# Loads, transform order and weight products at the head of a Fourier-mixing and leaky-ReLU kernel

## The chip, the cores and the metric

The kernel runs on one core of one Trainium2 chip. The metric is the time on the device in microseconds (us) for one launch. Times with L and a number refer to lines of the kernel before; TensorE is PE in the profile (its weight loads are PEld), VectorE is DVE, ScalarE is ACT, GpSimd is POOL and SyncE, which issues the DMAs, is SP.

## What is computed

The reference takes x of 8 batches of 3008 x 256 in fp32, forms the real part of its two-dimensional Fourier transform in each batch, and sends the 24064 rows of 256 through two weight matrices with a leaky ReLU between:

```python
X = np.fft.fft(x, axis=1)                 # x: (8, 3008, 256)
X = np.fft.fft(X, axis=2).real.astype(np.float32)
h = X.reshape(24064, 256) @ w_in          # (256, 2048)
g = np.maximum(0.01 * h, h)
out = g @ w_out                           # (2048, 256)
```

Both weight matrices come as 64-bit floats, and the kernel turns them into 32-bit floats itself.

## The kernel before, in words

**Stages.** The transform along the 256 features is never done on x. It is multiplied into the weights: a "weight product" (`fold_w_in`, L388) multiplies the table of feature cosines and sines (`feat_sb`) with w_in and leaves `wf`, whose two planes belong to the cosine and the sine part. The sequence transform remains. It uses mirror symmetries: `add_mirrors` (L241) adds a row block and its mirror image, `fold_columns` (L247 for the cosine part, L249 and a small memset at L250 for the sine part) folds the feature halves onto each other, and `fold_halves` (L257) adds or subtracts the halves of the sequence, for the even or odd output parity. What is left are small matmuls against tables: `sequence` (L416) does four with even rows (L431, 95 of the 128 partitions carry rows) and three with odd rows (L441). `butterfly` (L446) then combines the even and odd sums into the mixed rows: one copy on ScalarE (L452) and four operations on VectorE (L453 to L457). Feature column 128 has no partner; its transform (`nyquist`, from `nyx`, which holds all eight batches) goes the same way for 8 rows at once and is then spread over all partitions: for the first block by a matmul with a row of ones (`spread_first`, L516, and copies at L517), later through DRAM. For output parity 0 the rows are folded once more into quarters (`fold_quarters`, L274 to L280, six operations on VectorE and two copies on ScalarE).

**Blocks.** A batch and a parity make a unit; its 753 or 752 mixed columns are cut into three blocks of 251 or 250. For each block `up` (L532) multiplies by `wf` into two PSUM tiles, cos_ps and sin_ps (L538), VectorE adds the column-128 part and forms sums and differences (L543, L547, L548), and ScalarE applies the leaky ReLU (L549). `down` multiplies by w_out: `down_plain` (L581) for the first two blocks, a form with seven products in place of eight (L601), with sums made by GpSimd (L556 to L559), for all others. There are 48 blocks of 8 steps.

**The head.** Weights and the first batch arrive while the kernel already runs. Up to step 15 the order on VectorE, TensorE and SyncE is written out by hand (`manual_schedule`, L652), in an inner region on GpSimd too; ScalarE's order and everything after step 15 is placed by the framework's scheduler, which may also put later operations into earlier gaps. SyncE issues the DMAs of the head in one queue, at most eight in flight. `keep_warm` (L646) issues matmuls on zeros. A block of weights is converted in several VectorE operations, interleaved with the steps: `begin` (L343, L344, then L345 and L346 on ScalarE), `mantissa` (L351), `end` (L361, L362). w_in comes as 256, 256 and three times 512 columns, so there are five weight products; each writes its planes in PSUM tiles of the tag "up", of which there are four shared with cos_ps, sin_ps and the transforms, and ScalarE copies them to `wf` (L394). After the copy of the plane w=1, SyncE spreads one row of it to `wn` (L401), which L543 needs.

**The places that the steps touch.** In the inner region (L663 to L704): loads of x split into `evens` (four of seven row groups) and `odds`; fillers, Nyquist additions on GpSimd (L482 to L484), conversion and first weight product, fillers, column-128 transform, then row folds on VectorE, transforms of the first unit, spreading, and the first butterfly. Behind it the hand-written steps: `up(*steps[n])`, `down(*steps[n-2])`, conversions, and the weight products 2 to 5. [...]

Of the kernel before, what the change touches and what calls it, by code (L numbers as in the profile page):

```python
# [55 lines left out]
P = 128  # L56
# [3 lines left out]
NT = 7  # L60
# [144 lines left out]
def tile_fnet_leaky_relu(  # L205
# [99 lines left out]
    def load_tab(q, n, c):  # L305
        t = const.tile([P, TW[c][n % 2]], F32, name=f"tab_{n}_{c}")
        q.dma_start(t, seq_tab[n, c, :, 0 : TW[c][n % 2]])
        tabs[n, c] = t
# [79 lines left out]
    def fold_w_in(f0, n, made):  # L388

        for w in (1, 0):  # L390
            pt = up_ps()[:, 0:n]
            for a in range(2):
                nc.tensor.matmul(pt, lhsT=feat_sb[:, a, w * P : (w + 1) * P], rhs=made[a].dst, start=(a == 0), stop=(a == 1))  # L393
            nc.scalar.copy(wf[:, w, f0 : f0 + n], pt)  # L394
            if w == 1:
                spread_wn(f0, n)
# [19 lines left out]
    def sequence(rows, m, part, c):  # L416
# [3 lines left out]
        pe, po = dft_ps(), dft_ps()  # L420
        kf, kw = KF[c], KW[c]
        tab, n = tabs[2 * part, c], NI[0]
        for i in range(n):
            if c == 1:
                still, to = rows[0:PE_ROWS, i], pe[0:m, i % 2 * kf : (i % 2 + 1) * kf]
            else:
# [5 lines left out]
                             start=(i == 0), stop=(i == n - 1), skip_group_check=True)  # L432
        tab, n, at = tabs[2 * part + 1, c], NI[1], 0
# [10 lines left out]
        return pe, po  # L444
# [14 lines left out]
    def dft(u, blk):  # L459


        b, c = u
        if u in folded:
            rows = folded[u][blk]
        elif c == 1:
            rows = zs[b][:, 1 - blk, 0, :, blk * P : (blk + 1) * P]
        else:
            rows = quarters.pop((b, blk))
        sums = sequence(rows, P, blk, c)

        def rest():
            t = work.tile([P, UW[0]], F32, tag=f"mix{blk}", bufs=2, name=f"mix{blk}")
            butterfly(t, sums, P, blk, c)
            mixed.setdefault(u, {})[blk] = t
        return rest
# [10 lines left out]
    def nyquist(c):  # L486
        if c == 1:
            rows = nya[:, 1]
        else:
            halves = [nyb[:, 0], nyb[:, 1]]  # L490
            fold_quarters(nya[:, 0], halves, halves[0][:, 5], [h[:, 6] for h in halves])
            rows = halves, halves[0][:, 5]
        sums = sequence(rows, B, 0, c)

        def rest():
            t = work.tile([P, UW[0]], F32, tag="mix0", bufs=2, name="nyq")
            butterfly(t, sums, B, 0, c)
            nc.sync.dma_start(nyq_dram[:, c, 0 : UW[c]], t[0:B, 0 : UW[c]])
            return t
        return rest  # L500
# [116 lines left out]
    def step(at):  # L617
        if at < len(steps):
# [6 lines left out]
            if n == 0 and f in (2, 5):  # L625
                dft(units[1], f // 5)()
            if 0 < n < len(units) - 1 and f == 4:
# [4 lines left out]
                else:  # L632
                    dft(units[n + 1], part - 1)()
# [7 lines left out]

    def convert_w_in(f0, n, made):
        convert(made)
        fold_w_in(f0, n, made)
# [7 lines left out]
    with tc.manual_schedule(engines={mybir.EngineType.DVE, mybir.EngineType.PE, mybir.EngineType.SP}):  # L652
        with tc.manual_schedule(engines={mybir.EngineType.Pool}):
# [10 lines left out]

            def load_rows(h, rows):
                nc.sync.dma_start(t[:, h, :, rows], x[0, :, h, :, rows])
# [3 lines left out]
            load_rows(0, evens)  # L670
            nc.sync.dma_start(feat_sb, feat_tab.rearrange("(a p) n -> p a n", p=P))
            load_rows(1, evens)
            nc.sync.dma_start(nyx, x_nyq)
            for n in range(2):
                load_tab(nc.sync, n, 1)
            for h in range(2):
                load_rows(h, odds)
            for n in range(2, 4):
                load_tab(nc.sync, n, 1)
            o = load_w_out(0)  # L680
            keep_warm(10)
            fold_nyquist()
            convert_w_in(0, half, w)
            w, w1 = load_w_in(half, half), load_w_in(WN, WN)
            keep_warm(7)
            differences = work.tile([P, 4 * CW], F32, tag="s", bufs=4, name="differences")[:, 0 : NT * P].rearrange("p (c d) -> p c d", c=NT)
            nyq = nyquist(1)
            for rows in (evens, odds):
                for h in range(2):
                    add_mirrors(t, h, rows)  # L690
                    fold_columns(t, h, 0, rows)
                    if rows == odds and h == 0:
                        fold_columns(t, h, 1, slice(0, NT))
                fold_halves(t, 0, 1, rows, differences)
            fold_columns(t, 1, 1, slice(0, NT))
            fold_halves(t, 1, 1, slice(0, NT))
            zs[0] = t
            folded[units[0]] = differences, t[:, 0, 0, :, P:D]
# [96 lines left out]
```

## Time and profile before

The three timed runs have a median of 1932.13 us (1931.54 to 1933.2). The profiled execution has a span of 1930.8 us (1932.87 as timed). Its start, read from the timeline of the trace:

| what | start, us | length, us |
|---|---|---|
| fillers (L650), first piece | 1.09 | 6.08 |
| first weight product (L393) | 8.92 | 1.97 |
| fillers, second piece | 10.72 | 3.19 |
| column-128 transform (L431, then L441) | 13.84 | 1.44, then 2.06 from 15.12 |
| cosine rows, even (L431) | 17.11 | 1.54 |
| cosine rows, odd (L441) | 20.59 | 3.48 |
| sine rows, even (L431) | 23.86 | 1.82 |
| sine rows, odd (L441) | 25.52 | 2.06 |
| spreading (L516) | 27.51 | 1.52 |
| first product of the first block (L538) | 28.96 | 1.11 |

The weight products start at 8.92, 39.07, 51.88, 71.54 and 96.30 us. The transform of column 128 for parity 0 stands at 121.15 us on TensorE.

How to read it: lengths overlap, since matmuls are pipelined and their modelled ends lie after the start of the next. An fp32 matmul is two passes in the profile, so 8 passes are 4 matmuls. A time in square brackets behind a line is how long the engine had stood idle before it, and what ended that. "PEclk" is the clock granted to TensorE as a share of the full one. In the view by stretches the columns are busy time and number of instructions of each engine, then PEclk, the busy share of the DMA engines and the GB/s.

### The profile page before, as it was taken

Reading aid. Unit: us, or ns where it says so; the run is one execution under the profiler, and the core shown is the slowest. Engines: PE = TensorE matmul, PEld = TensorE weight load, DVE = VectorE, ACT = ScalarE, POOL = GpSimd, SP = SyncE. Lnnn points to the kernel's source line nnn. Section 1 sums busy time; section 2 is a strip of 40 time slices with the busy share of each in tenths; the row PEclk is TensorE's granted clock in tenths of the full one; section 3 lists DMA queues with packets and bytes.
Section 4 is the critical chain, followed back from the end, with each engine's and each line's share of the span. In section 5 each row is a group of like instructions: output and inputs, shape, how many; then the busy total and the mean of one; then the engine's idle time right before and its main releaser. Section 6 shows DMA issues by size and latency. Waiting matters only on the chain.

```text
span 1930.8 us, 24800 instructions
## 1 busy us (share of the span) xinstructions
PE 1918.1 (99%) x9040; PEld 1692.8 (88%) x9040; DVE 1157.2 (60%) x2273; ACT 468.7 (24%) x552; POOL 1061.4 (55%) x1513
## 2 busy tenths in 40 slices
PE   8999999999999999999999999999999999999999
PEld 6788888888888888888888888888888888888888
DVE  7868555584555755567555775558655585555554
ACT  3522222222222222222222222222222222222221
POOL 0136555575555755557555665556655575555554
PEclk9999999999999999999999999999999999999999
DMA  6202000110002000020000200002000020000000
GB/s 247 77 31 96 11 20 22 36 71 11 20 22 88 19 12 30 12 95 12 22 19 11 95 23 11 19 12 95 22 11 19 12 106 11 19 11 22 11 12 22
DMA packets 26728, 73.29 MB, mean 38 GB/s; under 512 B 4832, under 2 KB 17760, under 8 KB 24816
## 3 DMA queue, kind: packets, MB, share of 16 engines
q1 hardware_dynamic: 26608, 71.72, 10.0%
q8 instruction: 72, 1.18, 0.3%
q14 instruction: 48, 0.39, 0.1%
HBM read 46.99 MB, written 24.71 MB: 37 GB/s over the span
## 4 chain that ended last, share of the span: by engine, by line
PE 95%; DVE 3%; DMA 1%; issue 1%; ACT 0%; SPq 0%; DVEq 0%; ACTq 0%
PE sum_ps L601 55%; PE cos_ps L538 16%; PE sin_ps L538 16%; PE dft_ps L441 3%; PE sum_ps L581 3%; PE dft_ps L431 2%; DMA xt<-in_x_dram 1%; PE up_ps L393 1%; DVE cos L543 0%; DVE g L547 0%; DVE xt L241 0%; DVE g L548 0%; DVE xt L257 0%; DVE xt L247 0%; DVE xt L249 0%
## 5 line engine op out<-in xcount | busy, mean ns | idle before, releaser
L543 DVE SCALAR_TENSOR_TENSOR cos<-nb,wn,cos_ps 128x251 f32<-128x251 f32 (+1 forms) x768 | 330.6, 472 | 676.6 <-PE cos_ps L538 675.5
L549 ACT ACTIVATE g<-g 128x1004 f32<-128x1004 f32 (+1 forms) x384 | 399.2, 1040 | 1196.4 <-DVE g L548 1099.2
L556 POOL TENSOR_TENSOR s<-g 128x251 f32<-128x251 f32 (+1 forms) x368 | 268.1, 729 | 736.0 <-ACT g L549 736.0
L601 PE MATMUL sum_ps<-s,wt 128*128 128x251 f32 (+1 forms) x2208 | 528.0, 374 | 0.0
L601 PEld LDWEIGHTS sum_ps<-s,wt 128*128 128x128 f32 x2208 | 415.5, 188 | 53.2 <-issue 0.7
L538 PE MATMUL cos_ps<-mix,wf 128*128 128x251 f32 (+1 forms) x1536 | 388.4, 375 | 2.6 <-ACT wf L394 2.6
L538 PE MATMUL sin_ps<-mix,wf 128*128 128x251 f32 (+1 forms) x1536 | 387.8, 374 | 0.0
L601 PE MATMUL sum_ps<-g,wo 128*128 128x251 f32 (+1 forms) x1472 | 372.0, 374 | 0.8 <-DVE o L612 0.8
L538 PEld LDWEIGHTS cos_ps<-mix,wf 128*128 128x128 f32 x1536 | 290.8, 190 | 40.2 <-ACT wf L394 5.5
L538 PEld LDWEIGHTS sin_ps<-mix,wf 128*128 128x128 f32 x1536 | 290.4, 189 | 34.7
L601 PEld LDWEIGHTS sum_ps<-g,wo 128*128 128x128 f32 x1472 | 279.2, 190 | 40.6 <-DVE o L612 1.6
L559 POOL TENSOR_TENSOR s<-g,s 128x251 f32<-128x251 f32 (+1 forms) x368 | 273.2, 742 | 28.9
L547 DVE TENSOR_TENSOR g<-cos,sin_ps 128x502 f32<-128x502 f32 (+1 forms) x384 | 259.7, 676 | 47.0 <-DVE cos L543 10.3
L557 POOL TENSOR_TENSOR s<-s,g 128x251 f32<-128x251 f32 (+1 forms) x368 | 275.1, 748 | 0.0
L558 POOL TENSOR_TENSOR s<-g 128x251 f32<-128x251 f32 (+1 forms) x368 | 261.8, 712 | 0.0
L548 DVE TENSOR_TENSOR g<-cos,sin_ps 128x502 f32<-128x502 f32 (+1 forms) x384 | 257.2, 670 | 0.0
L601 PE MATMUL sum_ps<-s,wo 128*128 128x251 f32 (+1 forms) x736 | 215.8, 375 | 0.0
L601 PE MATMUL sum_ps<-g,wt 128*128 128x251 f32 (+1 forms) x736 | 215.8, 375 | 0.0
L601 PEld LDWEIGHTS sum_ps<-s,wo 128*128 128x128 f32 x736 | 139.5, 189 | 16.3
L601 PEld LDWEIGHTS sum_ps<-g,wt 128*128 128x128 f32 x736 | 139.8, 190 | 15.8
L612 DVE TENSOR_TENSOR o<-e,sum_ps 128x251 f32<-128x251 f32 (+1 forms) x184 | 67.5, 408 | 8.7 <-ACT e L610 8.7
L581 PE MATMUL sum_ps<-g,wo 128*128 128x251 f32 x256 | 57.1, 374 | 0.0
(75 smaller groups left out, 677.6 us busy)
## 6 DMA issues: line engine op xcount, KB each, us to landing
xt<-in_x_dram SPq DMA_DIRECT2D x14, 1792.0 KB, 9.3
out_dram<-o SPq DMA_DIRECT2D x80, 251.0 KB, 2.3
raw<-in_w_out_dram SPq DMA_DIRECT2D x8, 512.0 KB, 4.4
out_dram<-o SPq DMA_DIRECT2D x16, 250.0 KB, 2.1
raw<-in_w_in_dram SPq DMA_DIRECT2D x6, 512.0 KB, 4.4
nb<-nyq_dram SPq DMA_DIRECT2D x8, 376.5 KB, 3.4
nb<-nyq_dram SPq DMA_DIRECT2D x7, 376.0 KB
xt<-in_x_dram SPq DMA_DIRECT2D x2, 1024.0 KB, 7.6
```

Source lines behind the costliest of these rows:

```text
L538: nc.tensor.matmul(pt[blk][:, h * n : (h + 1) * n], lhsT=wf[:, blk, fs[h] * P : (fs[h] + 1) * P], rhs=mixed[b, c][blk][:, at : at + n], st ...
L543: nc.vector.scalar_tensor_tensor(cos[:, hs], in0=spreads[b, c][:, at : at + n], scalar=wn[:, fs[h] : fs[h] + 1], in1=pt[0][:, hs], op0=ALU ...
L547: nc.vector.tensor_tensor(g[:, 0], cos[:, 0 : 2 * n], pt[1][:, 0 : 2 * n], op=ALU.add)
L548: nc.vector.tensor_tensor(g[:, 1], cos[:, 0 : 2 * n], pt[1][:, 0 : 2 * n], op=ALU.subtract)
L549: nc.scalar.activation(g, g, ACT.Lrelu)
L556: nc.gpsimd.tensor_tensor(s1, a[1][0], a[1][1], op=ALU.add)
L557: nc.gpsimd.tensor_tensor(s2, s1, a[0][0], op=ALU.subtract)
L558: nc.gpsimd.tensor_tensor(s3, a[0][0], a[1][0], op=ALU.subtract)
L559: nc.gpsimd.tensor_tensor(s4, a[0][1], s2, op=ALU.subtract)
L581: nc.tensor.matmul(sums[j][d][:, r * n : (r + 1) * n], lhsT=wo[:, fs[h] // NH, fs[h] % NH, d * P : (d + 1) * P], rhs=a[r][h], start=(f == ...
L601: nc.tensor.matmul(sums[j][p], lhsT=still[p], rhs=moving[p], start=(f == 0 and i % 2 == 0), stop=(f == NH - 1), skip_group_check=True)
L612: nc.vector.tensor_tensor(to, x, y, op=ALU.add)
```

## The change

1. **Fewer bytes.** Of the even rows of the first batch and of the even tables only 96 of 128 partitions are loaded; GpSimd sets the other 32 partitions of the even rows to zero.
2. **Load order.** w_in, both even halves, the first even table, the feature table, column 128, both odd halves, the other three tables, w_out.
3. **Order in the head.** The Nyquist additions and the conversion come first, then all row folds on VectorE, with the sine folds of the even rows moved ahead of the odd rows. On TensorE the fillers are one piece of 20, before 10 and 7. Then even rows of column 128, even rows of the cosines, the first weight product, and after it the odd rows of both, then the sines. The weight product thus stands in the middle of the column-128 (d=128) transform; its PSUM tiles are now of the tag "sum". The loads of the next w_in blocks stay behind the weight product in SyncE's queue.
4. **Pieces.** Each weight product's plane w=0 is computed and copied in two pieces of half the columns, in one PSUM tile; the plane w=1 stays whole.
5. **Places of the weight products.** The fourth (from column 1024) moves from behind down(5) to before it, right behind up(7); the fifth moves from the start of step 12 to step 11, between up(11) and down(9).
6. **Tail.** Both `fold_halves` for parity 0 stand at step 14, before one each at 14 and 15. The quarter folds of the first batch and of column 128 for parity 0 are now the last things in the hand-written order.

The functions `sequence`, `dft` and `nyquist` are split so that the even and the odd rows can be called apart; the operations stay the same.

```diff
+    def load_tab(n, c):
+        rows = slice(0, (PE_ROWS + 1) if n % 2 == 0 else P)
         t = const.tile([P, TW[c][n % 2]], F32, name=f"tab_{n}_{c}")
-        q.dma_start(t, seq_tab[n, c, :, 0 : TW[c][n % 2]])
+        nc.sync.dma_start(t[rows], seq_tab[n, c, rows, 0 : TW[c][n % 2]])
...
-    def fold_w_in(f0, n, made):
-        for w in (1, 0):
-            pt = up_ps()[:, 0:n]
-            for a in range(2):
-                nc.tensor.matmul(pt, lhsT=feat_sb[:, a, w * P : (w + 1) * P], rhs=made[a].dst, start=(a == 0), stop=(a == 1))
-            nc.scalar.copy(wf[:, w, f0 : f0 + n], pt)
+    def fold_w_in(f0, n, made, tag="up"):
+        for w, pieces in ((1, 1), (0, 2)):
+            pt = ps.tile([P, 512], F32, tag=tag, bufs=4, name="wf_ps")
+            for piece in range(pieces):
+                cols = slice(piece * n // pieces, (piece + 1) * n // pieces)
+                for a in range(2):
+                    nc.tensor.matmul(pt[:, cols], lhsT=feat_sb[:, a, w * P : (w + 1) * P], rhs=made[a].dst[:, cols],
+                                     start=(a == 0 and piece == 0), stop=(a == 1), skip_group_check=True)
+                nc.scalar.copy(wf[:, w, f0 + cols.start : f0 + cols.stop], pt[:, cols])
...
+            nc.gpsimd.memset(t[PE_ROWS + 1 : P, :, :, evens], 0.0)
             def load_rows(h, rows):
-                nc.sync.dma_start(t[:, h, :, rows], x[0, :, h, :, rows])
+                used = slice(0, PE_ROWS + 1 if rows == evens else P)
+                nc.sync.dma_start(t[used, h, :, rows], x[0, used, h, :, rows])
...
             w = load_w_in(0, half)
-            load_rows(0, evens)
+            for h in range(2):
+                load_rows(h, evens)
+            load_tab(0, 1)
             nc.sync.dma_start(feat_sb, feat_tab.rearrange("(a p) n -> p a n", p=P))
-            load_rows(1, evens)
             nc.sync.dma_start(nyx, x_nyq)
-            for n in range(2):
-                load_tab(nc.sync, n, 1)
             for h in range(2):
                 load_rows(h, odds)
-            for n in range(2, 4):
-                load_tab(nc.sync, n, 1)
+            for n in range(1, 4):
+                load_tab(n, 1)
             o = load_w_out(0)
-            keep_warm(10)
             fold_nyquist()
-            convert_w_in(0, half, w)
-            w, w1 = load_w_in(half, half), load_w_in(WN, WN)
-            keep_warm(7)
+            convert(w)
...
-            nyq = nyquist(1)
             for rows in (evens, odds):
                 for h in range(2):
                     add_mirrors(t, h, rows)
                     fold_columns(t, h, 0, rows)
                     if rows == odds and h == 0:
-                        fold_columns(t, h, 1, slice(0, NT))
+                        fold_columns(t, h, 1, rows)
                 fold_halves(t, 0, 1, rows, differences)
-            fold_columns(t, 1, 1, slice(0, NT))
+                for h in range(2):
+                    if rows == evens or h == 1:
+                        fold_columns(t, h, 1, rows)
             fold_halves(t, 1, 1, slice(0, NT))
...
-            ready = [nyq, dft(units[0], 0), dft(units[0], 1)]
-            spread_first(ready[0]())
-            ready[1]()
+            keep_warm(20)
+            cosine, sine = ((rows_of(units[0], blk), P, blk, 1) for blk in range(2))
+            nyq = nyquist_rows(1), B, 0, 1
+            evens = [even_rows(*nyq), even_rows(*cosine)]
+            fold_w_in(0, half, w, "sum")
+            w, w1 = load_w_in(half, half), load_w_in(WN, WN)
+            sums_of_d128 = evens[0], odd_rows(*nyq)
+            sums_of_cosines = evens[1], odd_rows(*cosine)
+            sums_of_sines = even_rows(*sine), odd_rows(*sine)
+            spread_first(mix_nyquist(1, sums_of_d128))
+            mix(units[0], 0, sums_of_cosines)
             o.begin()
             o.mantissa()
-            ready[2]()
+            mix(units[0], 1, sums_of_sines)
...
         up(*steps[7])
+        fold_w_in(2 * WN, WN, w2)
         down(*steps[5])
-        fold_w_in(2 * WN, WN, w2)
...
-            if at == 12:
-                fold_w_in(3 * WN, WN, w3)
             if old is not None:
                 convert_on(old, new)
             up(*steps[at])
+            if at == 11:
+                fold_w_in(3 * WN, WN, w3)
             down(*steps[at - 2])
-            if at > 13:
-                fold_halves(t, at - 14, 0, slice(0, NT))
+            if at == 14:
+                for part in range(2):
+                    fold_halves(t, part, 0, slice(0, NT))
         done = 14
-    for part in range(2):
-        fold_x_quarters(0, part)
-    nyquist(0)()
+        for part in range(2):
+            fold_x_quarters(0, part)
+        nyq = nyquist_rows(0), B, 0, 0
+    mix_nyquist(0, (even_rows(*nyq), odd_rows(*nyq)))
```

## The prediction

> **What bounds the kernel now.** First the page, for the share of each engine; then the chain of waits over the first 160 us, for what sets the time where TensorE isn't full; then the timeline for each step of the change; then the stretch table for clock and bandwidth.
>
> ```profile
> PE 1918.1 (99%) x9040; PEld 1692.8 (88%) x9040; DVE 1157.2 (60%) x2273; ACT 468.7 (24%) x552; POOL 1061.4 (55%) x1513
> ```
>
> TensorE is busy all the time, and the change removes no useful matmul: it touches only the first 125 us. What it can win there is TensorE's idle and half-speed time, plus its filler matmuls; beyond, the chain is matmuls back to back, and any shift of the head reaches the end one to one. The chain shows where the head isn't matmul-bound:
>
> ```profile
> 15.84 0.97 DVE xt L241
> ...
> 20.59 3.48 PE dft_ps L441 x6
> 24.07 1.61 PE dft_ps L431 x8
> 25.68 1.90 PE dft_ps L441 x6
> 27.58 1.47 PE dft_ps L516 x4
> ...
> 71.70 3.45 PE up_ps L393 x8
> 75.17 0.59 ACT wf L394
> 75.81 1.11 PE cos_ps L538 x4
> ```
>
> Up to 20.6 us the last rows of x set the pace (the DMA before the first line ends at 15.8); then the transforms; and after each weight product (L393) TensorE waits for ScalarE's copy (L394). In the first L441 line six passes of 376 columns take 3.48 us; the third line shows 1.90 for the same six. The reason is in the stretch table (PEclk is the column after the busy times):
>
> ```profile
> 20.00:21.00 1.00, 0.41 (x2) 0.32 (x3) 1.00 (x2) 0.00 (x0) 0.00 (x0) 1.00 1.11 398
> 21.00:22.00 1.00, 1.00 (x4) 0.52 (x3) 0.90 (x2) 0.00 (x0) 0.00 (x0) 0.61 1.06 424
> 22.00:23.00 1.00, 1.00 (x3) 0.66 (x2) 1.00 (x3) 0.00 (x0) 0.00 (x0) 0.50 1.03 420
> ```
>
> After 1.94 us of idling the clock falls to half for about 3.4 us. The timeline gives the rest:
>
> ```profile
> 11.38 1.23 DVE L241 TENSOR_TENSOR xt<-xt 128x1024 f32<-128x1024 f32 x1 [1.28 <-DMA xt<-in_x_dram]
> 11.72 1.16 POOL L482 TENSOR_TENSOR nyx<-nyx 128x112 f32<-128x112 f32 x1 [10.54 <-DMA nyx<-in_x_nyq_dram]
> ...
> 20.59 3.48 PE L441 MATMUL dft_ps<-tab,differences 128*128 128x376 f32 x6 [1.94 <-DVE differences L257]
> ...
> 28.96 1.11 PE L538 MATMUL cos_ps<-mix,wf 128*128 128x251 f32 x4
> ...
> 68.14 3.56 PE L581 MATMUL sum_ps<-g,wo 128*128 128x251 f32 x16
> ...
> 70.97 0.69 DVE L362 SCALAR_TENSOR_TENSOR win<-win,power 128x512 f32<-128x512 f32 x1
> ...
> 71.54 3.59 PE L393 MATMUL up_ps<-win,feat_sb 128*128 128x512 f32 x8
> ```
>
> The fourth line is the first block's first product: its start, 28.96 us, measures the head. The last three matter most below: the third weight product starts right as its weights are finished on VectorE.
>
> **What the Trainium skill says.** (1) "TensorE: Matmul & The Clock Gate", Part 1, "What's actually happening": half rate after an idle window of about 3.4 us, full rate after a busy one, windows running freely. The trace agrees on the length (0.5 from 21.4 to 24.6), but idling 1.94 us was enough; 1.75 us before 8.92 was not. (2) "PSUM — Partial Sum Buffer", "PSUM bank collisions raise a hardware error": two engines must be kept apart by bank, not by address. The trace agrees as far as it goes: at 101.72 L543 begins on the first half of cos_ps only when both halves, in one bank, are done (100.57 + 1.11 = 101.68). (3) "DMA: Bandwidth & Descriptors", "Why a DMA increments its semaphore by 16 and not by 1": a 96-partition tile still goes to 16 engines. No run here shows such a load. (4) "SBUF — State Buffer", "Who interferes with whom": GpSimd and VectorE can lock each other out. L482 agrees: 1.16 us for 112 elements, ending 0.27 after L241, where its neighbours of 56 take 0.30.
>
> **The change part by part.** All from the profiled execution, whose span is 1930.8 us; the timed runs lie at 1932.13 (1931.54 to 1933.2). I add the difference to 1932.13.
>
> *Loads.* Each evens load falls from 1024 to 768 KB (96 of 128 rows), each even table from 376 to 282. Behind one another up to: evens 1280 and 2048 KB, first table 2330, nyx 2698, odds 3466 and 4234, second table 4798 (before: nyx 2928, odds 4636 and 5404). The stretch table has some 410 GB/s, 400 KB a us, from 8 us on. From the old ends (evens 1536 KB at 8.14, nyx 2928 at 11.72, odds 4636 at 15.84): evens 7.5 and 9.4, nyx 11.15, odds 13.1 and 14.8, second table 16.2. GpSimd's new memset writes 4096 elements on 32 partitions; `blank` took 0.31 for 256 and `one` 0.20 for 128, so about 3.5 us, over by 4.8, before anyone needs it; it only sits ahead of the Nyquist additions, which wait for 11.15. Bounds: 0, or 1.7 us later if rows rather than bytes set the load time (rival 3).
>
> *VectorE.* Conversion unchanged, ended 7.2. Then with the durations of the timeline (1024: 1.25, 768: 1.0, 512: 0.62, 384: 0.5): evens end 11.3, cosine difference 11.9, sine columns 13.1; odds 0 to 15.1; odds 1 and difference 17.1; sine halves 18.6. Before, the difference ended at 20.4 and sine at 22.5. Splitting two sine folds (2 x 1.0 into 2 x 0.62 + 2 x 0.48) adds 0.2, hidden in the wait for odds.
>
> *TensorE.* The 27 fillers become 20 in one piece, to 1.09 + 6.0 + 20 passes x 0.213 = 11.3. Nyquist additions end near 12.3 (three of 0.3 from 11.15, and turns with VectorE). From 12.4 all is there in time, so the chain is a sum: three even transforms at 1.28, three odd at 1.99, weight product 1.80, spreading 1.45 = 13.06, plus 0.62 for the cut product: its two pieces lie in one PSUM tile, so by (2) the second waits for the copy of the first (end of matmul 0.18, copy of 128 columns 0.26 by 0.37 for 256 and 0.59 for 512, signals 0.09, restart 0.09). The first block begins at 26.1 instead of 28.96: **-2.85**. No 1.9 us gap is left. The first L543 follows by 1.2, as before. Bounds -1 and -3.3. SP's weight loads, now behind the later wn copies, land before 24; w[0].begin wants them near 25.7. Hidden.
>
> *Second and third product (L393 at 39.07 and 51.88).* Before, the copy costs 0.80 and 0.95 (51.88 + 3.42 = 55.30 without it; 56.16, and 0.09 for the restart). Now a wait of 0.62 or 0.73 lies between the pieces, and ScalarE has its 0.72 us conversions (L345, L346) in the way. I take 0 for both; bounds -0.9 and +0.6 each.
>
> *Fourth product (w2), moved ahead of down(5).* VectorE's work isn't moved: w2[1] ends at 71.66, and VectorE has no idle from 57.31 to there. TensorE's up(7) ends at 68.14, where down(5) now hides the wait. After the change the product starts at 68.14, does the half with w2[0] to 69.0, and waits for w2[1] to 71.7: **2.7 us idle**, with down(5) queued behind. Counted from up(4) at 56.16: 15.55 to the weights, then 0.85 + 0.85, 0.73 between pieces, 0.85, down(5) 3.40: up(8) after 22.2 instead of 19.65 + 0.09: **+2.5** (+1.8 if pieces overlap). By (1) a gap longer than 1.94 should also halve the clock for 3.4 us; with 0.6 of that waiting, **+1.4** (0 to 1.7).
>
> *Fifth product (w3), moved to up(11).* Its weights end at 92.0, up(11) at 92.9: no wait. 0.95 becomes 0.73: -0.2 (bound -0.95).
>
> *Tail of the head.* Both sine and cosine halves at step 14 fall into VectorE's idle (2.87 and 1.00 us before 111.91 and 117.01). The Nyquist quarter folds, six of 0.16 at 13.6 to 15.4 now, come last in VectorE's written order. I take 0, if TensorE's order puts the block's next product first; bound below. Even tables of the second parity: fewer bytes, no waiter, 0.
>
> Sum: -2.85 + 0 + 2.5 + 1.4 - 0.2 = **+0.85**: 1933.0.
>
> **Rivals.** *1, faster: pieces overlap, clock stays.* For it: the columns are disjoint, and the gap may straddle two windows. Against: shared tile, and the 20.6 us gap. Head -3.45, second -0.8, third -0.95, fourth +1.85, fifth -0.95: -4.3, so 1927.8. *2, slower: the Nyquist transform of the even parity starves.* TensorE does it at 121.15, between steps 15 and 16. VectorE is full from 117.0; its last quarter fold ends at 122.87 and six Nyquist folds now follow, to about 123.3. If the order on TensorE stays, it idles 2.15 and the clock falls, 1.4: 1936.6. It decides when the folds end over 2 us after step 15. For it: the order in this trace. Against: code after the written-out region is placed by readiness, and up(16) could go first. *3: the change doesn't do what it says.* 96 rows take as long as 128, the head gains nothing, and the fourth product still costs: 1935.9. For it: six rows an engine is an untried shape; against: (3).
>
> **How the numbers follow.** Forecast 0.5 (own range 1930.5 to 1935.0); rival 1 0.17, rival 2 0.18, rival 3 0.15. About 0.2%, 3.9 us, is what a measurement can tell from no change. Below 1928.3 lies most of rival 1, with partly hidden copies: 0.14. Above 1936.0: most of rival 2, half of 3: 0.18. The rest, 0.68. The range 1928.0 to 1936.8 takes in the rivals but their outer halves.
>
> **What would show it.** Head: L538 first at 26.1, L441 on the differences near 1.9 us, and PEclk 1.0 there. Product: a PE wait on ScalarE inside L393. Fourth product: 2.7 us of TensorE waiting for L362, then clock 0.5. Nyquist: a wait for L280 near 118. I am wrong if that 2.7 us wait isn't there, or if the head gains under 1 us.

## The result, and the profile after

The changed kernel takes **1941.64 us** (median of four runs, 1940.83 to 1942.47) against 1932.66 (1931.54 to 1933.63) before: a ratio of 1.0047, 95% interval 1.0029 to 1.0064. It is some 9 us **slower**, and outside the range of the prediction (1933.0; 1928.0 to 1936.8). The profiled execution has a span of 1940.1 us, 9.3 over the one before.

From here on L numbers are those of the changed kernel: products L397 and their copies L399 (were L393, L394), even rows L435 (L431), odd rows L450 (L441), column-128 additions L491 to L493 (L482 to L484), the block's products L544 (L538), end of a weight conversion L363 (L362). Runs built on the kernel before have its numbers, shifted by what they add.

The page's first section shows a busy TensorE as before; 6.4 us more of it, and 26 more instructions:

```profile
PE 1924.5 (99%) x9066; PEld 1699.3 (88%) x9066; DVE 1158.1 (60%) x2275; ACT 468.8 (24%) x557; POOL 1064.3 (55%) x1516
```

A matmul counts as longer when the clock is low, so this row doesn't say what was lost. The chain of waits does (start, length, what):

```profile
3.76 10.09 DMA nyx<-in_x_nyq_dram
...
13.99 0.73 POOL nyx L491
...
14.79 0.64 POOL nyx L492
15.43 0.04 issue
15.47 5.48 PE dft_ps L435 x16
20.96 2.57 PE wf_ps L397 x8
...
25.01 4.08 PE dft_ps L450 x12
29.09 1.28 PE dft_ps L435 x8
```

Before, rows of x set the pace. Now one transfer of 112 KB, column 128, is under way for 10.09 us, and TensorE's first transform waits for it and for the two additions. The prediction had that transfer landing at 11.15 and the transform starting at 12.4; it started at 15.47. Then sixteen passes of L435 take 5.48 us, where eight take 1.28 further down: half speed again. The stretch table (columns as before) has both causes:

```profile
9.00:10.00 1.00, 1.00 (x6) 0.87 (x6) 0.96 (x2) 0.00 (x0) 0.00 (x0) 1.00 1.02 244
10.00:11.00 1.00, 1.00 (x7) 0.87 (x6) 0.58 (x1) 0.00 (x0) 0.00 (x0) 1.00 1.03 210
...
14.00:15.00 1.00, 0.00 (x0) 0.00 (x0) 1.00 (x2) 0.00 (x0) 0.92 (x2) 0.77 1.04 421
15.00:16.00 1.00, 0.53 (x2) 0.24 (x3) 1.00 (x3) 0.00 (x0) 1.00 (x2) 0.50 1.02 415
...
24.00:25.00 1.00, 1.00 (x5) 0.87 (x6) 0.00 (x0) 0.00 (x0) 0.00 (x0) 0.61 0.07 1
```

From 5 to 12 us, while the 96-row loads run, the DMA engines are as busy as ever (1.02) and move only 184 to 250 GB/s; from 13 to 18 us, with the odd rows on all partitions, they move 396 to 432. And from about 14.5 (0.77 over its slice) to 24.8 (0.61) the clock is at half: ten microseconds, where before it was 3.4. The timeline shows where the first block and the fourth weight product now stand:

```profile
15.47 2.68 PE L435 MATMUL dft_ps<-tab,nyx 95*8 95x188 f32 x8 [3.91 <-POOL nyx L492]
...
33.65 1.11 PE L544 MATMUL cos_ps<-mix,wf 128*128 128x251 f32 x4
...
74.01 1.12 PE L397 MATMUL wf_ps<-win,feat_sb 128*128 128x512 f32 x2
77.98 2.42 PE L397 MATMUL wf_ps<-win,feat_sb 128*128 128x512 f32 x6 [2.85 <-DVE win L363]
80.86 2.07 PE L397 MATMUL wf_ps<-win,feat_sb 128*128 128x256 f32 x4 [0.46 <-ACT wf L399]
```

Each row below takes the starts of two products of a block (the step's number in brackets) in both traces:

| stretch on TensorE | before | after | difference | predicted |
|---|---|---|---|---|
| start to up(0) | 28.96 | 33.65 | +4.69 | -2.85 |
| up(0) to up(2), second product | 12.62 | 12.79 | +0.17 | 0 |
| up(2) to up(4), third product | 14.58 | 15.21 | +0.63 | 0 |
| up(4) to up(7) | 10.28 | 10.51 | +0.23 | 0 |
| up(7) to up(8), fourth product | 9.37 | 14.02 | +4.65 | +3.9 |
| up(8) to up(11) | 15.39 | 15.28 | -0.11 | 0 |
| up(11) to up(12), fifth product | 9.37 | 9.58 | +0.21 | -0.2 |
| up(12) to the end | 1830.2 | 1829.1 | -1.1 | 0 |

The last row holds +0.3 around the column-128 transform, and the absence of two delays that the trace of before has, 0.8 us near 179 us and 0.6 us near 1118 us. Most other traces, those of x7, x11 and y1 among them, lack both delays too. So some 1.4 us by which such a run is shorter than before says nothing of its edit.

### The profile page after: what moved, and what is told of

The parts are those of the page before. It is cut to its first block, busy times and chain, and to the rows that moved or that the text cites. A ratio compares the mean times of both kernels' runs of the same rounds, so it can differ in the third digit from the quotient of the medians.

```text
span 1940.1 us, 24859 instructions
## 1 busy us (share of the span) xinstructions
PE 1924.5 (99%) x9066; PEld 1699.3 (88%) x9066; DVE 1158.1 (60%) x2275; ACT 468.8 (24%) x557; POOL 1064.3 (55%) x1516
## 3 DMA queue, kind: packets, MB, share of 16 engines
q1 hardware_dynamic: 26352, 70.90, 10.2%
## 4 chain that ended last, share of the span: by engine, by line
PE 97%; DVE 1%; DMA 1%; ACT 0%; SPq 0%; issue 0%; POOL 0%; DVEq 0%; POOLq 0%; ACTq 0%
PE sum_ps L607 56%; PE cos_ps L544 17%; PE sin_ps L544 17%; PE dft_ps L450 3%; PE sum_ps L587 2%; PE dft_ps L435 2%; PE wf_ps L397 1%; DMA nyx<-in_x_nyq_dram 1%; DMA wn<-wf 0%; DVE g L553 0%; DVE cos L549 0%; DVE g L554 0%; ACT wf L399 0%; ACT g L555 0%; DVE win L363 0%; DVE power L362 0%
## 5 line engine op out<-in xcount | busy, mean ns | idle before, releaser
L544 PE MATMUL cos_ps<-mix,wf 128*128 128x251 f32 (+1 forms) x1536 | 388.2, 375 | 0.0
L544 PE MATMUL sin_ps<-mix,wf 128*128 128x251 f32 (+1 forms) x1536 | 387.8, 374 | 0.0
L544 PEld LDWEIGHTS cos_ps<-mix,wf 128*128 128x128 f32 x1536 | 291.0, 190 | 35.0 <-issue 0.6
L544 PEld LDWEIGHTS sin_ps<-mix,wf 128*128 128x128 f32 x1536 | 290.4, 189 | 34.7
L563 POOL TENSOR_TENSOR s<-s,g 128x251 f32<-128x251 f32 (+1 forms) x368 | 279.5, 759 | 0.0
L554 DVE TENSOR_TENSOR g<-cos,sin_ps 128x502 f32<-128x502 f32 (+1 forms) x384 | 257.2, 670 | 0.0
```

The costliest lines, as they stand in the source:

```text
L544: nc.tensor.matmul(pt[blk][:, h * n : (h + 1) * n], lhsT=wf[:, blk, fs[h] * P : (fs[h] + 1) * P], rhs=mixed[b, c][blk][:, at : at + n], st ...
L554: nc.vector.tensor_tensor(g[:, 1], cos[:, 0 : 2 * n], pt[1][:, 0 : 2 * n], op=ALU.subtract)
L563: nc.gpsimd.tensor_tensor(s2, s1, a[0][0], op=ALU.subtract)
```

## The experiments

Most variants were run once, and the time stands beside that of the kernel before on the same chip, in brackets. Twenty runs of the kernel before spread over 3 us (1931.33 to 1934.54) and sixteen of y1 over 5, so a difference of 1 or 2 us between single totals says little. The argument rests on the starts in the traces.

**The load rate alone (x4_rates).** Kernel before, with the later batches' loads each cut in two by partitions:

```diff
-            nc.sync.dma_start(t[:, h], x[b, :, h])
+            if b == 1:
+                nc.sync.dma_start(t[0:96, h], x[b, 0:96, h])
+                nc.sync.dma_start(t[96:P, h], x[b, 96:P, h])
...
+            elif b == 3:
+                nc.sync.dma_start(t[0:112, h], x[b, 0:112, h])
+                nc.sync.dma_start(t[112:P, h], x[b, 112:P, h])
...
+            else:
+                nc.sync.dma_start(t[:, h], x[b, :, h])
```

> The kernel before, with the loads of the later batches of x, which are off the path, cut by partitions: batch 1 in 96 and 32 rows, batch 2 in 64 and 64, batch 3 in 112 and 16, batch 4 in 80 and 48, batch 5 in 32 and 96 (from partition 32), batches 6 and 7 whole. Each has the same bytes. Theory A (which partitions a transfer reaches sets its rate, not its bytes): whole batches land at 400 GB/s in 8.5 to 9 us for 3.6 MB, batch 2 at about 200 GB/s, batches 1, 3, 4 and 5 between, 200 to 320; the share of busy time of the DMA engines is near 1.0 in all. Theory B (the head's slow rate came from the mix with small loads, or from HBM at the start): all batches land at 380 to 410 GB/s. The time in all stays that of before, within 1 us, as long as the rows are there before their folds; one or two us more if not.

The stretch table of that run has, line by line, batch 1 (96 and 32 rows), batch 2 (64 and 64), batch 3 (112 and 16), batch 6 (whole):

```profile
160.00:161.00 1.00, 1.00 (x7) 0.90 (x6) 1.00 (x1) 0.57 (x1) 0.35 (x1) 1.00 1.03 244
...
390.00:391.00 1.00, 1.00 (x7) 0.90 (x6) 1.00 (x1) 0.33 (x1) 0.59 (x1) 1.00 1.06 215
...
620.00:621.00 1.00, 1.00 (x7) 0.90 (x6) 0.00 (x0) 0.57 (x1) 0.35 (x1) 1.00 1.27 258
...
1322.00:1323.00 1.00, 1.00 (x6) 0.90 (x6) 0.86 (x2) 0.00 (x0) 0.00 (x0) 1.00 1.04 416
```

Every batch that is cut, even into 112 and 16 rows, moves about half as much in these stretches, with the engines equally busy. The same 3.67 MB took 16.5 to 20.5 us from the first packet to the end of the last in the five cut batches, and 11 us in the two whole ones. In the head a packet of 4096 bytes took 159 ns (median) in the whole loads of the kernel before, and 281 in the 96-row loads of the changed one. So the slow rate goes with how many partitions a load covers, not with this kernel's head. Why it does isn't shown.

This run shows a second thing. Its head is that of the kernel before, and nothing fills the gap ahead of the odd cosine rows (here L457; the block's products are L554). Yet its rows came sooner, TensorE idled 1.37 us instead of 1.94, the clock stayed at 1.00, and the first block began 1.92 us earlier:

```profile
19.59 2.13 PE L457 MATMUL dft_ps<-tab,differences 128*128 128x376 f32 x6 [1.37 <-DVE differences L273]
...
27.04 1.11 PE L554 MATMUL cos_ps<-mix,wf 128*128 128x251 f32 x4
```

So a start in a single trace can move by 2 us through the loads and the clock alone.

**Fewer bytes alone (x8_before96).** Kernel before with 96-row loads and the memset of the change, its order untouched.

```diff
+        rows = slice(0, (PE_ROWS + 1) if n % 2 == 0 else P)
...
-        q.dma_start(t, seq_tab[n, c, :, 0 : TW[c][n % 2]])
+        q.dma_start(t[rows], seq_tab[n, c, rows, 0 : TW[c][n % 2]])
...
+            nc.gpsimd.memset(t[PE_ROWS + 1 : P, :, :, evens], 0.0)
...
-                nc.sync.dma_start(t[:, h, :, rows], x[0, :, h, :, rows])
+                used = slice(0, PE_ROWS + 1 if rows == evens else P)
+                nc.sync.dma_start(t[used, h, :, rows], x[0, used, h, :, rows])
```

> The kernel before with only the first part of the change: 96 of 128 rows for the even rows of x and the even tables, and the memset. The order of loads stays. Theory A (96-row transfers move 225 to 245 GB/s, so that each takes longer than its 128 rows did): the first even half lands near 9 us instead of 8.1, the second near 13 instead of 11.3, the odd ones near 18 instead of 15.8, the first product is 1.5 to 3 us later; 1934 to 1936 us. Theory B (bytes decide): all land earlier and the first product comes 1 us earlier or, with TensorE bound otherwise, stays; 1931 to 1932.5 us.

1936.1 against 1932.68: the part called "fewer bytes" costs 3.4 us by itself. The first block came 3.16 us later than before (32.12), after a wait of 3.00 for VectorE's difference.

**All rows in the changed kernel (x1_rows128).**

```diff
-        rows = slice(0, (PE_ROWS + 1) if n % 2 == 0 else P)
+        rows = slice(0, P)
...
-            nc.gpsimd.memset(t[PE_ROWS + 1 : P, :, :, evens], 0.0)
...
-                used = slice(0, PE_ROWS + 1 if rows == evens else P)
+                used = slice(0, P)
```

> The changed kernel with all 128 rows loaded again for the even rows of x and the even tables (no memset); load order and everything else as changed. Theory A (the transfers of 96 rows are slow: 244 GB/s with engines as busy as at 410): nyx lands at about 12.7 us instead of 13.9, although 704 KB more are moved, the first L435 starts near 13.9 instead of 15.5, and the first block's product near 28 us if the clock holds, near 30 if the 2.6 us gap still halves it; 1935 to 1938 us in all. Theory B (the new order of loads and transforms is the cause, whatever the rows): more bytes in front of nyx make it land at 14 us or later and the first product stays at 33 us or later; 1941 us or more.

1940.13 (1932.37), and the first block at 32.03, only 1.6 us sooner than in the changed kernel. The rate is back (371 to 418 GB/s from 7 to 13 us), but column 128 still comes late, since all rows ahead of it are more bytes:

```profile
13.45 0.87 POOL L491 TENSOR_TENSOR nyx<-nyx 128x112 f32<-128x112 f32 x1 [12.27 <-DMA nyx<-in_x_nyq_dram]
...
15.08 2.67 PE L435 MATMUL dft_ps<-tab,nyx 95*8 95x188 f32 x8 [3.52 <-POOL nyx L492]
```

The theory that slow rows alone are the cause fell here.

**Column 128 first (x9_nyx_first).** The changed kernel with its load right behind w_in.

```diff
             w = load_w_in(0, half)
+            nc.sync.dma_start(nyx, x_nyq)
...
-            nc.sync.dma_start(nyx, x_nyq)
```

> The changed kernel with column 128 (nyx, 112 KB) loaded right behind w_in, ahead of the even rows; nothing else. Theory A (the transforms start late because nyx lands behind the slow even rows and its additions then contend with VectorE): the additions are done before 10 us and take 0.3 us each for the smaller ones; the first L435 waits for its table instead, near 12.5 us, TensorE idles about 1.3 us, the clock holds, and the first product starts near 28 to 30 us instead of 33.6; 1937 us. Theory B (the even rows and their folds on VectorE bound the transforms, whenever nyx comes): even cosines still start after 16.5 us and the clock still falls; first product after 32.5 us, 1940 us or more.

1939.51 (1932.67). The additions are over by 8.56, and TensorE waits all the same:

```profile
15.62 2.67 PE L435 MATMUL dft_ps<-tab,nyx 95*8 95x188 f32 x8 [4.18 <-DMA tab<-in_seq_tab_dram]
```

Its other operand, the table, comes behind two slow even loads and is slow itself. So two causes cover each other: taking either away leaves the other at nearly the same time.

**Both at once (y1_rows_and_nyx)**: the edits of the last two together, run 16 times.

> The changed kernel with all 128 rows loaded and column 128 loaded right behind the first weights. Theory A: the slow rows and the late column 128 cover each other and are together the cause of the late start. Then column 128's additions are done before 9, the first even table lands near 13.4 (the place of column 128's load with all rows, since the bytes ahead are the same), the first transform starts at 13.3 to 13.8 instead of 15.47, and the first block's first product at about 28 if the clock holds (13.9 for the chain, as with 30 fillers), or 31.4 if it still falls to half after the 2 us of idle; total 1936 or 1939.3. Theory B: the new order itself costs. Then VectorE's folds of the even rows end after 16, the cosine transform waits for them 2 us or more behind the first transform, and the first product comes at 32 or later whatever the clock: 1940 or more.

Median 1936.89 (1935.02 to 1940.16), before 1932.4; ratio 1.0022, interval 1.0015 to 1.003.

```profile
14.25 1.43 PE L435 MATMUL dft_ps<-tab,nyx 95*8 95x188 f32 x8 [1.51 <-DMA tab<-in_seq_tab_dram]
...
28.70 1.11 PE L544 MATMUL cos_ps<-mix,wf 128*128 128x251 f32 x4
```

In this execution (1935.41 us) the clock stayed at 1.00 and the first block came at 28.70: all of the head's loss is gone, and no gain is left (28.96 before). The table was later than expected (14.2, not 13.4); from 4 to 9 us only 165 to 344 GB/s were moved. Theory A is upheld for the cause, not for the amount. The trace shows one of the shorter runs. Those with a mean clock of 1.000 took 1935.0 to 1935.4 us, those at 0.998 took 1936.8 to 1938.7, and the one at 0.997 took 1940.16: in most runs some clock is still lost, and no trace shows where.

**Holding the clock (x5_fill30).**

```diff
-            keep_warm(20)
+            keep_warm(30)
```

> The changed kernel with 30 filler matmuls instead of 20, so that TensorE is busy until about 15.6 us, when the additions for column 128 are done. Theory A (most of the lost head is the half clock that follows 3.9 us of idling): PEclk stays 1.0, the transforms take 13.7 us as predicted, the first block's product starts at 29.3 instead of 33.6, and the kernel takes 1937.3 us. Theory B (the clock is lowered by the 8-column matmuls of column 128, or by the heavy mix of the head, not by the idling): the clock falls all the same and the first product stays later than 32 us; 1940.5 us or more.

1937.85 (1932.68). TensorE had no gap, the clock stayed at 1.00 in the head, and the chain from first transform to first block was as the prediction had summed it:

```profile
16.08 1.44 PE L435 MATMUL dft_ps<-tab,nyx 95*8 95x188 f32 x8
...
30.01 1.11 PE L544 MATMUL cos_ps<-mix,wf 128*128 128x251 f32 x4
```

13.93 us here (13.7 predicted), 18.18 in the changed kernel: the half clock costs 4.25 us, of which 0.6 is given back because the fillers end later. Part of the 4.25 is chance. In x2 (below) the head is that of the changed kernel and its first transform starts at the same 15.47, but the half clock lasted 6.8 us instead of 10.2, and the first block came at 32.63 instead of 33.65.

**The same in the kernel before (x7_gap_fill)**: five fillers between the even and odd cosine rows, where it idles 1.94 us.

```diff
+        if m == P and part == 0 and c == 1 and not mixed:
+            keep_warm(5)
```

> The kernel before with five filler matmuls (2.1 us) between the even and the odd cosine rows, where TensorE idles 1.94 us. Theory A (the idling halves the clock): PEclk stays 1.0 from 20 to 25 us, the odd cosines take 2.0 instead of 3.5 us, and the first product comes 1.3 to 1.6 us earlier; 1930.8 us. Theory B (the clock falls for another reason there): the fillers only fill, 0 to 0.4 us slower; 1932.5 us.

1931.35 (1932.68), clock at 1.00, odd cosine rows in 2.06 instead of 3.48. The loads came 0.9 us later in this run, so the start of the first block (28.91) shows less than the clock gave. The total doesn't speak for the fillers: at step 16 this run is level with before (123.14 against 123.18), and what it gains is the two late delays. Nor does it show that the fillers held the clock, since x4 held it without them. What it shows is the price of the half clock, 1.4 us on these six passes.

**One piece (x3_one_piece).**

```diff
-        for w, pieces in ((1, 1), (0, 2)):
+        for w, pieces in ((1, 1), (0, 1)):
```

> The changed kernel with each weight product's plane w=0 in one piece, all else as changed. Theory A (pieces in one PSUM tile add waits): the third product loses its wait for ScalarE, the fourth and fifth lose 0.5 to 0.7 each since their copy lies behind other work anyway, the head loses 0.35, the second is unchanged; 1939.5 to 1940.5 us. Theory B (pieces hide the copies): the waits ahead of up(2) and up(4) come back at 0.8 to 0.95 each, 1 us slower; 1942.5 us.

1936.91 (1932.37), faster than both theories said. Part of that is chance: in the head the half clock lasted 6.8 us instead of 10.2, and at the fourth product, which still waited, the clock stayed up this time:

```profile
75.81 2.84 PE L397 MATMUL wf_ps<-win,feat_sb 128*128 128x512 f32 x6 [2.55 <-DVE win L363]
```

The stretch table of the same run, just behind that wait:

```profile
77.00:78.00 1.00, 1.00 (x3) 0.38 (x2) 1.00 (x3) 0.62 (x2) 0.00 (x0) 1.00 0.98 332
```

The fifth product at its new place, whole, costs nothing: up(11) to up(12) is 8.53, against 9.37 before and 9.58 with pieces.

**The fourth product back behind down(5) (x2_w2_back).**

```diff
         up(*steps[7])
-        fold_w_in(2 * WN, WN, w2)
         down(*steps[5])
+        fold_w_in(2 * WN, WN, w2)
```

> The changed kernel with the fourth weight product back behind down(5). Theory A (it waits for VectorE's weights, and the wait halves the clock): the 3.1 us wait inside it and the half clock after it go, up(8) comes 4 to 4.7 us earlier; 1937.2 us. Theory B (what costs there is the waiting between pieces and the copy on ScalarE, not the weights): under 1.5 us; 1940 us or more.

1936.23 (1932.37). No wait for L363, up(7) to up(8) in 9.82 instead of 14.02. Inside the third, fourth and fifth product TensorE still waits 1.11, 1.01 and 0.77 for the copy between the pieces.

**A tile for each piece (x10_own_tiles)**: x2 with the PSUM tile made inside the loop over pieces.

```diff
         for w, pieces in ((1, 1), (0, 2)):
-            pt = ps.tile([P, 512], F32, tag=tag, bufs=4, name="wf_ps")
             for piece in range(pieces):
+                pt = ps.tile([P, 512], F32, tag=tag, bufs=4, name="wf_ps")
...
-                                     start=(a == 0 and piece == 0), stop=(a == 1), skip_group_check=True)
+                                     start=(a == 0), stop=(a == 1), skip_group_check=True)
```

> As the run with the fourth product behind down(5), but each piece of a product has its own PSUM tile, so its own bank. Theory A (the second piece waits for the copy of the first because they lie in one bank): no wait of TensorE for L399 inside the products; 0.35 us in the head and at the second product, 1.0 to 1.1 at the third and fourth, 0.8 at the fifth come back; 3 us less than that run's 1936.2, 1933.2 us. Theory B (the framework or ScalarE's order makes the wait, not the bank): the waits stay; 1936 us.

1932.35 (1932.67), 3.9 less than x2. The twelve passes of each product now run without a break:

```profile
73.85 3.60 PE L397 MATMUL wf_ps<-win,feat_sb 128*128 128x512 f32 x12
77.29 1.01 PE L544 MATMUL cos_ps<-mix,wf 128*128 128x251 f32 x4
```

up(7) to up(8) is 8.54 us, with nothing lost. It was the shared tile that made the pieces wait; whether the framework asks for the wait by tile or by bank isn't separated.

**Rows, pieces, place and fillers together (x6_combo_fill)**: the edits of x1, x3, x2 and x5 in one kernel.

> The changed kernel with 128 rows in all loads, one piece in each product, the fourth product back behind down(5), and 30 fillers. What is left of the change is the order of loads and transforms in the head, the place of the fifth product and the tail. Theory A (slow 96-row loads, the half clock, the pieces and the fourth product's place are the whole loss): first product at 28.3 to 28.8 us against 28.96 before, 0.85 gained at the fifth product; 1930.5 to 1931.5 us. Theory B (the new order itself is a loss beyond these): first product after 29.5 us; 1932.5 us or more.

1933.05 (1932.68), with the first product at 30.50. These are theory B's numbers, but the trace gives another reason than the order: the fillers ran to 17.2, past the additions (15.2), and pushed the first transform to 17.21. Too many of them cost what they save.

**Places in the kernel before (x11_places)**: from step 8 on.

```diff
-            if at == 12:
-                fold_w_in(3 * WN, WN, w3)
...
-            up(*steps[at])
             down(*steps[at - 2])
+            up(*steps[at])
+            if at == 11:
+                fold_w_in(3 * WN, WN, w3)
```

> The kernel before with two weight products in other places: from step 8 on down(at-2) goes ahead of up(at), so that down(6) lies between the fourth product and up(8), and the fifth product stands behind up(11), ahead of down(10). Theory A (a product costs its copy, 0.95 us, only if the next up follows it, and nothing if its weights are ready): both copies are hidden, 0.85 to 0.95 each; 1930.7 us. Theory B (VectorE gets its step later by down's 3.4 us and the fifth product's weights come late, as the fourth's did in the changed kernel): at least one wait of 1 to 3 us for L362; 1933 us or more.

1929.23 (1932.67), better than either theory said. A block's down work now stands between a product and its reader, so ScalarE's copy is hidden in the fourth and fifth product, 0.84 us each. Of the 3.3 us between the profiled spans, 2.0 are there at step 16; the rest is the two late delays.

**Two versions from these findings.** x12_best has the load order of before with all rows, three fillers in the gap of x7, VectorE's order from the change, whole products, and the places of x11. y2_all_mended keeps the change's order of transforms, with all rows, column 128 first, 26 fillers, a tile for each piece and the same places; its edits are those of x1, x9, x2, x10 and x11, and

```diff
-            keep_warm(20)
+            keep_warm(26)
```

x12 differs from the kernel before, besides what is named above, by

```diff
+            cosine_evens = even_rows(*cosine)
+            keep_warm(3)
+            sums_of_cosines = cosine_evens, odd_rows(*cosine)
```

> What the runs point to: loads of 128 rows in the order of before; TensorE's order of before with three fillers between even and odd cosines; VectorE's order of the change (sine folds of the even rows ahead of the odd ones, Nyquist quarter folds behind step 15); whole products; down ahead of up from step 8 on, and the fifth product behind up(11). Theory A (idling and half clock, and the copies, are what can be won): first product 1.5 to 2.3 us earlier than before, two copies hidden for 1.8; 1928 to 1929.5 us, faster than both. Theory B (the head is bound by its loads alone): first product as before; 1930.5 to 1931 us.

> The changed kernel with all rows, column 128 first, 26 fillers in place of 20, a PSUM tile for each piece, the fourth product behind down(5), from step 8 on down ahead of up, and the fifth product behind up(11). Theory A: the new order of transforms is as good as the old one once its data are there and the clock holds: first product of the first block at 27.0 to 28.0 and the total 1929 to 1930 (1929.47 with 26.80 in the version with the old order; no wait of TensorE for the copies of the pieces takes up to 0.8 more off twice). Theory B: the weight product in the middle of the transform costs in itself: first product at 29 or later, total over 1930.5.

x12: 1929.47 (1927.83 to 1930.7), before 1932.67; ratio 0.9982, interval 0.9975 to 0.999. y2: 1928.27 (1927.64 to 1929.22), before 1932.4; ratio 0.998, interval 0.9971 to 0.9988. Both beat both kernels. What the fillers and VectorE's order add in x12 isn't shown: x11, the places alone, took 1929.23 in its one run, and x4's first block came at 27.04 with the head of before, where x12's came at 26.80. In y2 the first block starts at 28.78, later than forecast, although the total is below the forecast. The 26 fillers run to 15.5 and hide whatever was ready sooner:

```profile
1.69 13.86 PE L652 MATMUL sum_ps<-blank 128*128 128x256 f32 x51
15.47 1.44 PE L435 MATMUL dft_ps<-tab,nyx 95*8 95x188 f32 x8
```

From there its chain takes 13.31 us, 0.6 less than x5's, as no copy is waited for. So the weight product in the middle adds no wait to the chain. Whether the order as a whole is as good as the old one stays open: with y1's start of 14.25, this chain would put the first block at 27.56, which is an estimate, and x12's comes at 26.80. Its weight product is done from 8.77 on, while rows are under way.

## Why the prediction was wrong

**The step that failed is "Loads".** It priced 96-row loads by their bytes, at the 400 KB a us of the whole loads, and so had column 128 landed at 11.15; it landed at 13.85. The Trainium skill, "DMA: Bandwidth & Descriptors", section "Why a DMA increments its semaphore by 16 and not by 1", says that 96 partitions still go to 16 engines; the trace agrees that all are busy (1.02), but that isn't a rate, and the measured one is 184 to 250 GB/s. I took a statement on how many engines work for one on how fast they are, without a row of this kernel to support it. Rival 3 named the shape as untried and gave it no worse than the time of 128 rows; it is worse, by 3.4 us in the kernel before (x8). (Its terms add up to 1935.8, not 1935.9.)

**The additions** were to end near 12.3. They began at 13.99, 2.84 late by the transfer, and took 0.73, 0.63 and 0.74 where I had 0.3 each: VectorE no longer waits for rows there, it runs its folds back to back, and GpSimd gives way; in x9, where the additions come ahead of the folds, they took 0.54, 0.36 and 0.30. I had written "turns with VectorE" and counted nothing for it.

**"No 1.9 us gap is left"** fell with these two: the gap is 3.9 us, and the clock was at half for ten. Of the 7.54 us between forecast and result at the first block, 3.07 are the later start and 4.25 the clock (x5), 1.0 of it by chance (x2); the chain itself was right to 0.2. Of the prediction's two signs of being wrong, a head that gains under 1 us came true; the wait at the fourth product was there, 2.85 us for 2.7.

**The gain of 2.85** was seen in no run. The best start that this order showed with its data waited for is y1's 14.25, 1.8 us after the forecast's 12.4, and it comes out level with before. But y1 isn't the forecast with its rate put right: it moves 3048 KB up to the first table, 350 more than the forecast had up to column 128, and from 4 to 9 us below the 400 KB a us. Whether 96 rows at that rate would have gained 2.85 us stays unknown, since no run moves them at it.

**Fourth product:** right in kind, +4.65 against +3.9. y1 splits it, as its clock stayed up: up(7) to up(8) is 12.66 there, 3.29 over before for the waits (2.5 forecast), and 1.36 more with the clock (1.4 forecast). That the clock fell was in part luck: at this product it fell in the changed kernel, x1 and x5, and held in x3, x9 and y1. **Second** right; **third** at its bound, ScalarE's conversions standing between the copies; **fifth** +0.2 for -0.2: pieces in one tile give up what the new place wins. The PSUM step, that the second piece waits for the copy of the first, is shown by x10. **Tail:** 0, as taken; rival 2's wait was 0.23 us instead of 2.15, because six of down(14)'s passes were put ahead of the transform. Rival 1 lost both its premises.

**What stays open.** Why the half clock lasted so long although TensorE had work from 15.5 on. It lasted three steps of 3.41 us (see the last section) in the changed kernel and x9, and two in x1, x2, x3 and x10, which also have the new order and a gap ahead of it. Four of the steps after which it stayed at half had no idling at all (17.96 to 21.37 in the changed kernel, and one each in x9, x2 and x3). They held even transforms (L435, on 95 rows) and at most 0.62 us of the weight product; in all six traces the clock rose after the first step with 0.98 us of it or more. That was seen, not tested. Open, too, is whether fewer fillers than 26 in y2 would win another microsecond: they weren't tried, and the loads arrive up to 0.9 us earlier or later from run to run.

## What to carry to other kernels

Price a load by a load of the same shape; leaving out partitions can make it slower in total, and one run of another part of the kernel with that shape settles it. When a start waits for several things, mend all of them in one run before concluding that one doesn't matter. Cut a product into pieces only with a PSUM tile for each, and put other work between a product and its first reader rather than the product ahead of its weights. Look at the clock in several traces before you book its loss or its gain: the same head ran at half clock for 6.8 us in one run and for 10.2 in another.

## What was not expected of the hardware

- A batch of x in loads of 112 and 16, 96 and 32, 80 and 48, or 64 and 64 partitions took 16.5 to 20.5 us (x4; 215 to 258 GB/s in the stretches shown), with the DMA engines fully busy; in loads of 128 it took 11 us (416 to 459 GB/s in full stretches).
- A GpSimd memset of 32 x 4096 elements (3.51 us from 1.23) held up VectorE's first conversion: L344 took 1.04 us instead of 0.29 and ended at 4.89, 0.15 after the memset. In six other runs with the memset it took 1.12 to 1.33 and ended at 4.89 as well; without it (x1) it took 0.29 again.
- The clock changes on a grid of 3.41 us. Worked out from the slices in which PEclk changes, the changed kernel's changes lie at 14.55, 24.79, 79.40 and 82.81 us, which are 3, 16 and 1 steps apart. In the kernel before, the slices of 0.61 and 0.68 put them at 21.22 and 24.64, one step (the prediction read 21.4 to 24.6). In every trace the changes lie whole steps apart, but the grid lies elsewhere in each. What counts, by these traces, is how much idling falls in one step, not how long the gap is. The same wait at the fourth product lowered the clock in x5 (first line), with 2.18 us of it in one step, and did not in x9 (second line), with 1.23 in one and 1.29 in the next:

```profile
73.45 3.50 PE L397 MATMUL wf_ps<-win,feat_sb 128*128 128x512 f32 x6 [2.52 <-DVE win L363]
77.02 1.99 PE L397 MATMUL wf_ps<-win,feat_sb 128*128 128x512 f32 x6 [2.52 <-DVE win L363]
```

Over all traces no step with 1.94 us of idling or more kept the full clock, and steps with up to 1.68 us kept it, but for one of 1.54 in x11. The Trainium skill, "TensorE: Matmul & The Clock Gate", Part 1, has windows that run freely, and these runs agree. A step needn't be idle throughout: 1.54, 1.94 and 1.99 us of 3.41 were enough here.
